# Retention attention and a PReLU feed-forward on one core: w_in's middle tiles loaded and cast in smaller pieces, three loads cut at partition 120

## The chip, the cores and the metric

The kernel runs on one core of a Trainium2 chip. A core has a matrix engine (TensorE, in the profile PE, its weight loads PEld), a vector engine (VectorE, DVE), a scalar engine (ScalarE, ACT), a general engine (GpSimd, POOL) and a sync engine (SyncE, SP), which issues most of the transfers between main memory and the on-chip memory of 128 partitions. Sixteen DMA engines carry these transfers. Each engine runs its own instructions in order and waits on semaphores for the others. The metric is device time in microseconds (us), lower is better; the kernel before was run three times.

## The reference

The reference computes retention attention for 4 batches, 8 heads, 768 positions and head size 64, and puts its result through a feed-forward layer.

```python
gamma = 1.0 - 2.0 ** (-5.0 - np.arange(H, dtype=np.float32))
scale = 1.0 / np.sqrt(D)
for t in range(S):
    state = gamma[None, :, None, None] * state + np.einsum('bhd,bhe->bhde', k[:, :, t], v[:, :, t])
    y[:, :, t] = scale * np.einsum('bhd,bhde->bhe', q[:, :, t], state)
...
x = np.ascontiguousarray(attn_out.transpose(0, 2, 1, 3)).reshape(B * S, H * D)
...
h = x @ w_in
g = np.maximum(h, 0.0) + alpha * np.minimum(h, 0.0)
return (g @ w_out).astype(np.float32)
```

There are 3072 tokens; w_in is 512 x 2048, w_out 2048 x 512, both in float32, as are all inputs.

## The kernel before

The attention is done in chunks. The 3072 positions are cut into 12 units (u = 0 to 11) of 256 positions, three to a batch. For each unit, `load` (L143) brings k, q and v in float32 as tiles ks, qs and vs. `rescale` (L182) multiplies k and q by powers of gamma and writes them as float16 into the tile kdq; `cast_v` makes the float16 tile vx. `turn_pe` (L222) transposes kdq on PE, eight 128 x 128 pieces for one half of the heads, first those of k and then those of q, into a bank of the accumulator (trb), and ACT copies it to the tile kq. `score_mm`, `masks`, `sum_mm`, `state` and `out_mm` then compute scores, masked scores, the unit's contribution to the state, the state, and the attention's output, which is stored transposed as xT.

The feed-forward works on blocks of two units (512 tokens). `ffn1` (L615) multiplies w_in's sixteen column tiles of 128 with xT, four matmuls to a tile and 512 tokens (hps, L629); ACT and DVE then apply the PReLU, into the tile gt. For block 0 it starts with tiles 0 to 3 for one unit at a time (`apart=4`), and goes on with tiles 4 to 15 in order. `ffn2` multiplies gt with w_out (ops). From block 1 on, seven products in place of eight are used for the second matrix.

The order on each engine is written by hand: the code is laid out in the order in which each engine is to do it, and `tick(gen, m)` puts m matmuls of a feed-forward generator between pieces of the attention. So PE has unit 2's transposes (`turn_pe(2, 0, 5)`, L1082) five matmuls after the end of block 0's `ffn1`, and cannot go on until POOL has rescaled unit 2's k and q.

The change concerns how w_in gets in. `get_wi(lo, hi)` (L960) issues on SP one transfer with tiles lo to hi - 1, into a staging buffer named early that `win_part` (L956) picks: tiles 0-3 and 12-15 share one place, so loads of tiles 12-15 have to wait until tiles 0-3 have been cast. `cast_wi` (L963) converts a range to float16 on POOL, into w_in_all (win). In the program's order SP issues: units 0 and 1; w_in 0, 1, 2-3, 4-5, 6-7, 8-11, 12-13, 14-15; then unit 2 (two halves of k, q, v). POOL does: cast 0, 1, 2-3, 4-5, 6-7; issue of w_out's first quarter (`get_wo(0)`, tile wout, converted on the way); cast 8-9, 10-11, 12-15; rescale of unit 2's k for heads 0-3; issue of w_out's second quarter; k for heads 4-7; q; cast of v. SP's transfers report on eight semaphores in turn, so each transfer is issued only when the one eight places earlier has landed.

Of the kernel before, what the change touches and what calls it, by code (L numbers as in the profile page):

```python
# [22 lines left out]
def kernel(  # L23
# [10 lines left out]
    nc = tc.nc  # L34
# [105 lines left out]
    def rows(x):  # L140
        return slice(64 * x, 64 * x + 64)

    def load(u, parts="kqv"):  # L143
        if u >= NU:
            return
        b, c = divmod(u, UPB)
        t = staged.setdefault(u, {})
        for nm in parts:
            src = {"k": k, "q": q, "v": v}[nm[0]]
            if nm[0] not in t:  # L150
                t[nm[0]] = sbp.tile(
                    [128, H, 2 * D], FP, tag=f"{nm[0]}s", bufs=3, name=f"{nm[0]}s{u}"
                )
            h = slice(0, H) if len(nm) == 1 else slice(4 * int(nm[1]), 4 * int(nm[1]) + 4)
            if u >= SPLIT and nm != "q":
                for x in range(2):
                    for y in range(2):
                        at = U * c + 128 * x + 64 * y
                        nc.sync.dma_start(
                            out=t[nm][rows(x), :, D * y : D * y + D],  # L160
                            in_=src[b, :, at : at + 64, :].rearrange("h p d -> p h d"),
                        )
                continue
            hold(
                nc.sync.dma_start(  # L165
                    out=t[nm[0]][:, h, :],
                    in_=src[b, h, U * c : U * c + U, :].rearrange(
                        "h (p r) d -> p h (r d)", r=2
                    ),
                )  # L170
            )
# [10 lines left out]
    def rescale(eng, u, t, h0, h1):  # L182
        kdq = unit(u)[0]
        at = OQ if t else (O2 if u >= SPLIT else 0)
        return eng.tensor_tensor(  # L185
            out=kdq[:, t, :, h0:h1, :].rearrange("p r h d -> p h r d"),
            in0=staged[u]["kq"[t]][:, h0:h1, :].rearrange("p h (r d) -> p h r d", r=2),
            in1=tab[:, at + 2 * h0 : at + 2 * h1]
            .rearrange("p (h r) -> p h r", r=2)
            .unsqueeze(3)  # L190
            .to_broadcast([128, h1 - h0, 2, D]),
            op=MULT,
        )
# [759 lines left out]
    wi = moe_w_in.rearrange("(hp p) d -> p hp d", p=128)  # L953
    wo = moe_w_out.rearrange("(ft p) d -> p ft d", p=128)

    def win_part(lo, hi):  # L956
        x, y = ((1, 0), (1, 1), (0, 0), (1, 0))[lo // 4]
        return early[x][:, y, :, 128 * (lo % 4) : 128 * (hi - lo + lo % 4)]

    def get_wi(lo, hi):  # L960
        nc.sync.dma_start(out=win_part(lo, hi), in_=wi[:, :, 128 * lo : 128 * hi])  # L961

    def cast_wi(eng, lo, hi):  # L963
        o, i = w_in_all[:, :, 128 * lo : 128 * hi], win_part(lo, hi)
        if eng is nc.scalar:
            return eng.activation(out=o, in_=i, func=COPY, bias=0.0, scale=1.0)
        return eng.tensor_copy(out=o, in_=i)  # L967
# [6 lines left out]
    V, G, A = nc.vector, nc.gpsimd, nc.scalar  # L974
# [1 line left out]
    nc.scalar.dma_start(out=alpha_sb, in_=moe_alpha.rearrange("(ft p) -> ft p", p=128))  # L976
    load(0, ("k0", "q0", "k1", "q1", "v0", "v1"))
    load(1, ("k0", "q0", "k1", "q1", "v0", "v1"))
    for lo, hi in ((0, 1), (1, 2), (2, 4), (4, 6), (6, 8), (8, 12)):
        get_wi(lo, hi)  # L980
    V.memset(spin, 1.0)
    V.memset(mi, 1.0)
# [3 lines left out]
        out=ident, in_=ident, pattern=[[-1, 128]], compare_op=EQUAL, fill=0.0,  # L986
# [4 lines left out]
        out=m, in_=m, pattern=[[-1, 2], [1, 2], [2, 64]], compare_op=NOT_LESS,  # L991
        fill=0.0, base=0, channel_multiplier=-2,
    )
    for lo, n in ((0, 64), (256, 32)):
        m = mj[rows(0), lo : lo + 4 * n].rearrange("p (a i t) -> p a i t", a=2, i=2)
        G.affine_select(
            out=m, in_=m, pattern=[[0, 2], [1, 2], [2, n]], compare_op=NOT_LESS,
# [7 lines left out]
        out=mi[rows(1), 0:640], in_=mi[rows(0), 0:640], func=COPY, bias=0.0, scale=1.0  # L1005
# [13 lines left out]
        out=aps[:, 0:NFT], in_=alpha_sb, identity=tab[0:NFT, OI : OI + NFT]  # L1019
# [3 lines left out]
        out=oma_sb, in0=aps[:, 0:NFT], scalar1=-1.0, scalar2=1.0, op0=MULT, op1=ADD  # L1023
# [26 lines left out]
    state(1, 0, V, "ga")  # L1050
    cast_wi(G, 2, 4)
    get_wi(12, 14)
    get_wi(14, 16)
    load(2, ("k0", "k1", "q", "v"))
    score_mm(1, 1, (0, 1))
# [6 lines left out]
    get_wo(0)  # L1062
    cast_wi(G, 8, 10)
    cast_wi(G, 10, 12)
    cast_wi(G, 12, 16)
    rescale(G, 2, 0, 0, 4)
    get_wo(1)
    rescale(G, 2, 0, 4, 8)
# [225 lines left out]
```

## Time and profile before

| | before |
|---|---|
| median of three runs | 199.02 us (198.73 to 199.23) |
| span of the profiled execution | 199.2 us (its own time is not given beside it) |
| PE busy | 190.3 us, 96% |
| DVE, ACT, POOL busy | 156.4, 114.5, 105.1 us |
| read from and written to main memory | 27.31 MB, 6.29 MB |
| granted TensorE clock | 1.000 over the span |

The span runs from the first to the last instruction. The busy time of an engine says little on the end by itself: what counts is which engine waits for what in which stretch. In the rows of the time line, the first number is the start in us from the span's start, the second the duration; xN says how many instructions are merged; in brackets stands how long the engine was idle before and what ended that. SPq rows are issues on SP: their duration is that of the issue, not of the transfer.

### The profile page before, as it was taken

The page shows a single profiled execution, that of the slowest core. Times are in us where ns is not written, and L with a number is a line of the kernel's source. Part 1 is how long each engine was busy: PE and PEld are TensorE (multiplying, and loading weights), DVE is VectorE, ACT ScalarE, POOL GpSimd, SP SyncE. Part 2 cuts the span into 40 slices and gives each one's busy share as a digit, 9 for nine tenths or more (in the row PEclk, how much of TensorE's full clock was granted, in tenths as well). Part 3 has the DMA queues.
Part 4 walks back from the last instruction along what each step waited for, and adds up shares of the span by engine and source line. Part 5 has one row for each costly group of instructions (what it writes and reads, how often), then busy time and mean ns, then how long its engine had stood idle before and what let it go on. Part 6 is the DMA issues. An engine that isn't in the chain of part 4 may idle for free.

```text
span 199.2 us, 6049 instructions
## 1 busy us (share of the span) xinstructions
PE 190.3 (96%) x2517; PEld 128.1 (64%) x2517; DVE 156.4 (79%) x258; ACT 114.5 (57%) x197; POOL 105.1 (53%) x111
## 2 busy tenths in 40 slices
PE   6788979899999999999999999999999999999993
PEld 2456524458548588844598744688644788865882
DVE  6699977236788999379989289987389998899983
ACT  4455754437368658476557576557476476688110
POOL 3197678389477724990067990066980081039400
PEclk9999999999999999999999999999999999999999
DMA  5999996999978999899786999916975110400014
GB/s 156 325 328 368 376 252 144 246 253 161 229 174 198 244 236 243 223 321 200 167 204 174 294 194 211 240 60 143 328 120 127 29 56 3 158 3 0 0 53 158
DMA packets 89449, 36.85 MB, mean 185 GB/s; under 512 B 57920, under 2 KB 87632, under 8 KB 89424
## 3 DMA queue, kind: packets, MB, share of 16 engines
q1 hardware_dynamic: 87136, 34.35, 66.2%
q0 software_dynamic: 2112, 2.10, 6.7%
q8 instruction: 19, 0.31, 0.6%
q10 hardware_dynamic: 176, 0.04, 0.2%
q14 instruction: 6, 0.05, 0.1%
HBM read 27.31 MB, written 6.29 MB: 169 GB/s over the span
## 4 chain that ended last, share of the span: by engine, by line
PE 80%; DMA 9%; SPq 5%; POOL 3%; ACT 1%; issue 1%; DVE 0%
PE hps L629 28%; PE ox L846 16%; PE oy L846 13%; PE ops L798 7%; DMA ks<-in_k_dram 6%; SPq L165 4%; PE hps L712 3%; DMA early<-in_moe_w_in_dram 3%; PE sp L752 3%; POOL kdq L185 2%; PE trb L230 1%; PE st L284 1%; PE y L532 1%; PE sca L465 1%; PE ov L846 1%; SPq L961 1%
## 5 line engine op out<-in xcount | busy, mean ns | idle before, releaser
L629 PE MATMUL hps<-xT,win 128*128 128x512 f16 (+1 forms) x384 | 71.3, 344 | 1.5 <-POOL win L967 1.5
L642 DVE SCALAR_TENSOR_TENSOR gt<-hm,oma,hps 128x512 f16<-128x512 f32 (+1 forms) x96 | 59.5, 655 | 15.2 <-ACT hm L640 6.5
L640 ACT ACTIVATE hm<-hps 128x512 f32<-128x512 f32 x80 | 47.6, 597 | 27.6 <-PE hps L629 25.6
L629 PEld LDWEIGHTS <-win 128*128 128x128 f16 x384 | 37.1, 98 | 33.4 <-POOL win L967 2.6
L846 PEld LDWEIGHTS <-gs 128*128 128x128 f16 x320 | 31.0, 98 | 3.7
L846 PEld LDWEIGHTS <-gt 128*128 128x128 f16 x240 | 22.8, 98 | 4.2
L333 POOL CAST tg<-tm 64x256 f16<-64x256 f32 x12 | 4.8, 396 | 35.0 <-DVE tm L301 22.5
L185 POOL TENSOR_TENSOR kdq<-ks,tab 128x1024 f16<-128x1024 f32 (+1 forms) x12 | 20.2, 1687 | 3.6 <-DMA vs<-in_v_dram 2.6
L185 POOL TENSOR_TENSOR kdq<-qs,tab 128x1024 f16<-128x1024 f32 (+1 forms) x11 | 20.1, 1823 | 2.7 <-DVE wsum L571 2.3
L846 PE MATMUL ox<-wout,gt 128*128 128x256 f16 x144 | 17.3, 273 | 0.0
L555 ACT ACTIVATE xT<-y 128x512 f16<-128x512 f32 x22 | 14.9, 743 | 4.0 <-PE y L532 3.0
L846 PE MATMUL oy<-wsum,gs 128*128 128x256 f16 x144 | 17.2, 272 | 0.0
L201 POOL CAST vx<-vs 128x1024 f16<-128x1024 f32 (+1 forms) x13 | 12.5, 970 | 5.5 <-DMA vs<-in_v_dram 5.5
L798 PE MATMUL ops<-wout,gt 128*128 128x512 f16 x64 | 15.3, 380 | 0.0
L612 DVE TENSOR_TENSOR gs<-gt 128x1024 f16<-128x1024 f16 (+1 forms) x14 | 13.0, 933 | 0.2
L866 ACT ACTIVATE cu<-oy 128x512 f32<-128x512 f32 x10 | 6.0, 597 | 10.6 <-PE oy L846 10.1
L236 ACT ACTIVATE kq<-trb 128x1024 f16<-128x1024 f16 x8 | 8.2, 1023 | 6.7 <-PE trb L230 6.6
L313 POOL TENSOR_TENSOR tf<-ss,tab 128x256 f32<-128x256 f32 x10 | 10.3, 1028 | 2.5 <-DVE ss L312 1.3
L662 POOL TENSOR_SCALAR hn<-qc,oma 128x256 f32<-128x256 f32 x4 | 4.5, 1139 | 12.5 <-DVE qc L774 12.4
L423 POOL TENSOR_TENSOR tf<-ss,tab 128x256 f32<-128x256 f32 x6 | 5.8, 974 | 9.1 <-DVE ss L422 9.1
L870 DVE TENSOR_TENSOR os<-ox,cu 128x512 f32<-128x512 f32 x5 | 3.4, 687 | 9.1 <-PE ox L846 9.1
L967 POOL CAST win<-early 128x1024 f16<-128x1024 f32 (+2 forms) x8 | 8.2, 1039 | 3.7 <-DMA early<-in_moe_w_in_dram 3.6
(116 smaller groups left out, 289.2 us busy)
## 6 DMA issues: line engine op xcount, KB each, us to landing
qs<-in_q_dram SPq DMA_DIRECT2D x10, 512.0 KB, 4.7
ks<-in_k_dram SPq DMA_DIRECT2D x32, 128.0 KB, 3.4
vs<-in_v_dram SPq DMA_DIRECT2D x32, 128.0 KB, 4.3
early<-in_moe_w_in_dram SPq DMA_DIRECT2D x5, 512.0 KB, 7.6
out_dram<-os SPq DMA_DIRECT2D x9, 256.0 KB, 2.6
wout<-in_moe_w_out_dram POOLq DMA_DIRECT2D x4, 512.0 KB, 6.4
out_dram<-ot SPq DMA_DIRECT2D x4, 512.0 KB, 3.6
ks<-in_k_dram SPq DMA_DIRECT2D x6, 256.0 KB, 4.8
```

What stands on the lines that cost most here:

```text
L185: return eng.tensor_tensor(out=kdq[:, t, :, h0:h1, :].rearrange("p r h d -> p h r d"), in0=staged[u]["kq"[t]][:, h0:h1, :].rearrange("p h ...
L201: eng.tensor_copy(out=o, in_=i)
L236: nc.scalar.activation(out=kq.rearrange("p (x a) i -> p x a i", x=4)[:, :, 2 * hh : 2 * hh + 2, :], in_=trb.rearrange("p (x a i) -> p x a ...
L313: nc.gpsimd.tensor_tensor(out=t, in0=ss, in1=dec, op=MULT)
L555: nc.scalar.activation(out=o, in_=i, func=COPY, bias=0.0, scale=1.0,)
L612: last_g.append(nc.vector.tensor_tensor(out=o, in0=a, in1=b, op=op))
L629: nc.tensor.matmul(out=hps[:, f, :].rearrange("p (u t) -> p u t", t=U), lhsT=w_in_all[:, hp, 128 * (f0 + f) : 128 * (f0 + f) + 128], rhs=x ...
L640: nc.scalar.activation(out=hm, in_=hps, func=RELU, bias=0.0, scale=-1.0)
L642: nc.vector.scalar_tensor_tensor(out=gt[:, f0 + f, U * lo : U * hi], in0=hm[:, f, :], scalar=oma_sb[:, f0 + f : f0 + f + 1], in1=hps[:, f, :],
L798: nc.tensor.matmul(out=opss[tq], lhsT=gt[:, ft, 128 * tq : 128 * tq + 128], rhs=w_out_all[:, ft, :], start=(ft == 0), stop=(ft == NFT - 1),)
L846: nc.tensor.matmul(out=o[1][m], lhsT=lhs(f, m), rhs=rhs(f), start=(first and f == 0 and (m == 0 or o[0] is None)), stop=(f == HF - 1), ski ...
L967: return eng.tensor_copy(out=o, in_=i)
```

## The change

Tiles 8-11 are loaded by two transfers, 8-9 and 10-11, in place of one. The cast of tiles 12-15 becomes two instructions. The loads of tiles 6-7, 10-11 and 14-15 are each made by two transfers, one for partitions 0 to 119 and one for partitions 120 to 127. Nothing else is changed; the bytes moved and what is computed are the same.

```diff
     def get_wi(lo, hi):
-        nc.sync.dma_start(out=win_part(lo, hi), in_=wi[:, :, 128 * lo : 128 * hi])
+        for p0, p1 in ((0, 120), (120, 128)) if lo in (6, 10, 14) else ((0, 128),):
+            nc.sync.dma_start(
+                out=win_part(lo, hi)[p0:p1], in_=wi[p0:p1, :, 128 * lo : 128 * hi]
+            )
...
-    for lo, hi in ((0, 1), (1, 2), (2, 4), (4, 6), (6, 8), (8, 12)):
+    for lo, hi in ((0, 1), (1, 2), (2, 4), (4, 6), (6, 8), (8, 10), (10, 12)):
         get_wi(lo, hi)
...
     cast_wi(G, 8, 10)
     cast_wi(G, 10, 12)
-    cast_wi(G, 12, 16)
+    cast_wi(G, 12, 14)
+    cast_wi(G, 14, 16)
     rescale(G, 2, 0, 0, 4)
```

On SP, from the load of tiles 6-7 to unit 2's loads, the program before has these transfers. DMAHW0 to DMAHW7 are the eight semaphores of the transfers, Pool is POOL's own; a wait that an earlier one covers is left out by the compiler.

```order
L961 DMA early<-in_moe_w_in_dram 128x4x256 [waits DMAHW2_49]
L961 DMA early<-in_moe_w_in_dram 128x4x512 [waits DMAHW3_49]
L961 DMA early<-in_moe_w_in_dram 128x4x256 [waits DMAHW6_49,DMAHW7_49,DMAHW4_49,Pool_49]
L961 DMA early<-in_moe_w_in_dram 128x4x256 [waits DMAHW5_49,DMAHW0_49,Pool_49]
L165 DMA ks_390<-in_k_dram 128x4x128 x2
L165 DMA qs_393<-in_q_dram 128x8x128
L165 DMA vs_395<-in_v_dram 128x8x128 [waits DMAHW1_49]
```

The same place now:

```order
L962 DMA early<-in_moe_w_in_dram 120x4x256 [waits DMAHW2_49]
L962 DMA early<-in_moe_w_in_dram 8x4x256 [waits DMAHW3_49]
L962 DMA early<-in_moe_w_in_dram 128x4x256 [waits DMAHW4_49]
L962 DMA early<-in_moe_w_in_dram 120x4x256 [waits DMAHW5_49]
L962 DMA early<-in_moe_w_in_dram 8x4x256 [waits DMAHW6_49]
L962 DMA early<-in_moe_w_in_dram 128x4x256 [waits DMAHW7_49,Pool_49]
L962 DMA early<-in_moe_w_in_dram 120x4x256 [waits DMAHW0_49,Pool_49]
L962 DMA early<-in_moe_w_in_dram 8x4x256 [waits DMAHW1_49]
L165 DMA ks_394<-in_k_dram 128x4x128 [waits DMAHW2_49]
L165 DMA ks_394<-in_k_dram 128x4x128 [waits DMAHW3_49]
L165 DMA qs_397<-in_q_dram 128x8x128 [waits DMAHW4_49]
L165 DMA vs_399<-in_v_dram 128x8x128 [waits DMAHW5_49]
```

Four transfers stand ahead of unit 2's k that did not stand there, and both halves of k and the q now wait for a transfer eight places back: k's halves for the two parts of tiles 6-7, q for tiles 8-9, v for the first part of tiles 10-11.

On POOL, from w_out's first issue to the rescale of unit 2's k, before:

```order
L971 DMA wout<-in_moe_w_out_dram 128x4x512
L967 CAST win<-early 128x4x256 [waits DMAHW3_49]
L967 CAST win<-early 128x4x256
L967 CAST win<-early 128x4x512 [waits DMAHW5_49,DMAHW4_49]
L185 TENSOR_TENSOR kdq_440<-ks_390,tab 128x4x2x64 [waits DMAHW6_49]
```

And now:

```order
L974 DMA wout<-in_moe_w_out_dram 128x4x512
L970 CAST win<-early 128x4x256 [waits DMAHW4_49]
L970 CAST win<-early 128x4x256 [waits DMAHW6_49,DMAHW5_49]
L970 CAST win<-early 128x4x256 [waits DMAHW7_49]
L970 CAST win<-early 128x4x256 [waits DMAHW1_49,DMAHW0_49]
L185 TENSOR_TENSOR kdq_445<-ks_394,tab 128x4x2x64 [waits DMAHW2_49]
```

Each cast of two tiles now waits for its own load alone; before, tiles 8-9 waited for the load of four, and tiles 12-13 for that of 14-15.

## The prediction

> **What bounds the kernel now.** I read the page first: TensorE (PE) is busy for 96% of the span and most of the chain that ended last.
>
> ```profile
> span 199.2 us, 6049 instructions
> PE 190.3 (96%) x2517; PEld 128.1 (64%) x2517; DVE 156.4 (79%) x258; ACT 114.5 (57%) x197; POOL 105.1 (53%) x111
> ...
> GB/s 156 325 328 368 376 252 144 246 253 161 229 174 198 244 236 243 223 321 200 167 204 174 294 194 211 240 60 143 328 120 127 29 56 3 158 3 0 0 53 158
> ...
> q8 instruction: 19, 0.31, 0.6%
> ...
> PE 80%; DMA 9%; SPq 5%; POOL 3%; ACT 1%; issue 1%; DVE 0%
> ```
>
> Only an edit that removes PE idle time can pay, so I asked next where PE is idle: a table of stretches (us, then busy time of PE, PEld, DVE, ACT and POOL with counts, granted clock, DMA share, GB/s).
>
> ```profile
> 18.00:36.00 18.00, 15.78 (x102) 8.05 (x96) 13.87 (x23) 10.15 (x18) 13.60 (x14) 1.00 0.98 269
> 36.00:60.00 24.00, 24.00 (x322) 14.74 (x321) 14.03 (x26) 12.45 (x20) 15.59 (x12) 1.00 0.96 214
> 60.00:84.00 24.00, 24.00 (x386) 19.50 (x384) 19.02 (x34) 16.51 (x30) 15.42 (x14) 1.00 0.96 226
> ```
>
> From 36 us on PE has no idle time and full clock; from 18 to 36 us it lacks 18.00 - 15.78 = 2.22 us. This is block 0's first matrix product, which runs beside the loads of w_in that the change touches. PE and POOL there, in order of time (start, duration, idle before and what ended it):
>
> ```profile
> 18.79 6.29 PE L629 MATMUL hps<-xT,win 128*128 128x256 f16 x40 [0.30 <-POOL win L967]
> 25.61 3.63 PE L629 MATMUL hps<-xT,win 128*128 128x512 f16 x16 [0.53 <-POOL win L967]
> 29.88 3.63 PE L629 MATMUL hps<-xT,win 128*128 128x512 f16 x16 [0.64 <-POOL win L967]
> 33.34 1.24 PE L798 MATMUL ops<-wout,gt 128*128 128x512 f16 x5
> 34.42 0.39 PE L230 MATMUL trb<-mi,kdq 128*128 128x128 f16 x4
> 35.56 0.40 PE L230 MATMUL trb<-mi,kdq 128*128 128x128 f16 x4 [0.75 <-POOL kdq L185]
> ```
>
> ```profile
> 19.98 2.02 POOL L967 CAST win<-early 128x1024 f16<-128x1024 f32 x2
> 21.95 0.99 POOL L971 DMA_DIRECT2D wout<-in_moe_w_out_dram  x1
> 24.52 2.02 POOL L967 CAST win<-early 128x1024 f16<-128x1024 f32 x2 [1.57 <-DMA early<-in_moe_w_in_dram]
> 27.93 1.89 POOL L967 CAST win<-early 128x2048 f16<-128x2048 f32 x1 [1.39 <-DMA early<-in_moe_w_in_dram]
> 30.78 1.04 POOL L185 TENSOR_TENSOR kdq<-ks,tab 128x512 f16<-128x512 f32 x1 [0.95 <-DMA ks<-in_k_dram]
> 31.77 0.81 POOL L971 DMA_DIRECT2D wout<-in_moe_w_out_dram  x1
> 32.59 1.06 POOL L185 TENSOR_TENSOR kdq<-ks,tab 128x512 f16<-128x512 f32 x1
> 33.60 1.90 POOL L185 TENSOR_TENSOR kdq<-qs,tab 128x1024 f16<-128x1024 f32 x1
> ```
>
> PE waits four times for POOL: 0.30 (tiles 2-3), 0.53 (tiles 8-9), 0.64 (tiles 12-15), 0.75 (unit 2's second transposes, which need its rescaled q). POOL in turn waits three times for a landing. The chain that ended last names only the last of these and what is behind it:
>
> ```profile
> 18.76 0.37 SPq L961
> ...
> 19.17 11.53 DMA ks<-in_k_dram
> 30.70 0.08 issue
> 30.78 1.04 POOL kdq L185
> ```
>
> So k of unit 2 lands at 30.70 and everything up to PE's 35.56 hangs on it; the cast waits ahead of it are not on the chain. Without an earlier k, time saved at 25.61 and 29.88 is only waited for at 35.56. Why is k so late? The bytes ahead of it are k, q, v of units 0 and 1 (6 x 0.524 MB), w_in (4.194 MB) and its own 0.262: 7.60 MB. The GB/s row, in slices of 4.98 us, sums over five slices (156 + 325 + 328 + 368 + 376) to 1553 x 4.98 us = 7.73 MB at 24.9 us. The sixteen DMA engines together had moved that much by then, and k was whole 5.8 us later. It isn't mean bandwidth, then, but single engines. No view prints each engine's share, but the trace holds the sixteen increments with which each load reports its landing (us; the packet times are medians of the same record):
>
> ```
> load                 first  15th   last   last - 15th
> k half 0 of unit 0    3.39   4.05   4.11   0.06
> w_in tiles 4-5       16.65  18.42  19.00   0.58
> w_in tiles 6-7       18.28  19.82  20.41   0.59
> w_in tiles 8-11      20.86  22.37  24.46   2.09
> w_in tiles 12-13     22.22  23.69  25.72   2.03
> w_in tiles 14-15     23.59  25.07  27.81   2.74
> k half 0 of unit 2   24.33  25.86  30.70   4.84
> q of unit 2          29.14  30.74  33.01   2.27
> packets: 1 KB 46 ns, 2 KB 84 ns; one 16 KB packet on q8, at 21.50 for 931 ns
> ```
>
> Fifteen shares of k are there at 25.86; one engine brings the last at 30.70. The instruction fetch (q8 above, a single packet of one engine) falls in the stretch where the lag jumps from 0.59 to 2.09, and w_out's first load, issued at 21.95, shares the late engine after 25 us while the others have already finished k.
>
> **The change part by part.** *Three loads (tiles 6-7, 10-11, 14-15) as 120 + 8 partitions.* A load of 128 partitions goes to sixteen engines, eight partitions (32 packets of 1 KB) each. If the shares stay whole, 120 partitions make fifteen, and one engine gets nothing: 3 x 32 x 46 ns = 4.42 us less for it ahead of unit 2's k. The eight remaining partitions are one more for up to eight engines: 3 x 4 x 46 ns = 0.55 us. The other seven are untouched.
>
> *Tiles 8-11 as two loads.* The packets halve: 32 x 84 = 2.69 us per engine become 64 x 46 = 2.94, +0.25 us on every engine. Tiles 8-9 land one load earlier.
>
> *Cast of 12-15 as two.* 1.89 us against 2.02 for two (the row of two at 24.52): +0.13 us for POOL, beside PE, and PE needs only the first ahead of tile 12.
>
> *SP.* Four issues more, at 0.37 to 1.19 us each:
>
> ```profile
> L961 SPq DMA_DIRECT2D early<-in_moe_w_in_dram x8: 368/692/1191, 9.9 to 18.8; - x8
> ```
>
> ```profile
> 14.04 1.05 SPq L961 DMA_DIRECT2D early<-in_moe_w_in_dram  x1
> ```
>
> ```profile
> 16.36 0.37 SPq L961 DMA_DIRECT2D early<-in_moe_w_in_dram  x1
> ```
>
> SP is free from 15.09 to 16.36 and from 16.73 to 18.76 (it waits there for POOL's casts to free the buffers), 3.30 us, against 4 x 0.69 = 2.76: hidden. The last load's second part is issued behind 18.76, and since eight completion counters go round, unit 2's k now waits until tiles 6-7 have landed, about 20.0 instead of an issue at 19.17. Its cover is the queue: tiles 14-15 keep fifteen engines busy until 25. A gap would need an issue later than that. I cost it at nothing (bounds: 0 to the 0.8 us of delay).
>
> *What follows if the spared engine is the late one.* Tiles 8-9 land at about 19.82 + 32 x 46 ns + up to 0.18 = 21.5, so POOL casts 8-9 and 10-11 right behind w_out's issue, from 22.95 to 24.97; 12-13 land at 23.69 + 0.25 + 0.37 = 24.3 and are cast by 26.0; 14-15 land at 25.07 + 0.25 + 0.55 = 25.9 and are cast by 27.0. PE asks for tile 8 at 25.08, for 10 at 26.8, 12 at 28.6, 14 at 30.3: the waits of 0.53 and 0.64 go, 1.17 us. Then PE is at unit 2's second transposes at 34.81 - 1.17 = 33.64 (34.42 + 0.39 is where it stops now). k lands at 25.86 + 0.80 = 26.7 at the latest, its second half 0.75 later. POOL: first half of k to 28.1, w_out's second issue to 28.9, second half to 29.9, then q. q's fifteenth share landed at 30.74; + 0.80 gives 31.5 and the rescale (1.90) ends by 33.5, just ahead of PE. The 0.75 goes too. Between the ends (q at 31.5, or still at 33.01 as before) I take the first: the last share was the late engine's.
>
> Behind 36 us the next step of POOL waits for DVE, which waits for PE's sums, so the shift should be kept:
>
> ```profile
> 40.65 0.61 POOL L423 TENSOR_TENSOR tf<-ss,tab 128x256 f32<-128x256 f32 x1 [4.17 <-DVE ss L422]
> ```
>
> Sum: 0.53 + 0.64 + 0.75 = 1.92 us. The profiled span is 199.2, 0.2 above the median of 199.02, with no time of its own shown; 199.02 - 1.92 = **197.1 us**.
>
> The rows do not name the late engine. [...]
>
> [...]
>
> **The rivals.** *The late engine is among the eight that get more.* Then k lands 0.55 + 0.25 = 0.80 us later than 30.70, POOL's chain behind it takes the same 4.8 us, and PE's last wait ends at 36.36: 199.02 + 0.80 = 199.8 us, more if w_out's packets cost the late engine again. It decides as soon as k's landing moves past 30.70. [...]
>
> *It is one of the seven untouched, or the split spares nobody.* The cast waits go, the wait at the transposes grows by as much: 199.0 to 199.3 us. [...]
>
> *The engine is spared, but w_out's loads hold q back.* w_out's second issue moves from 31.77 to about 28, and its packets run beside q and v. With q at 32.5 PE would go on at 34.45 instead of 33.64: 197.9 us; with q at 33.0, 198.4.
>
> **How the numbers follow.** Forecast 0.64, q held back 0.10, nothing spared 0.11, ninth partition on the late engine 0.15. About 0.3% (0.6 us) is what a measurement of this kernel can tell from no change: the first two are faster (0.74), the third the same (0.11), the fourth slower (0.15). The likeliest case alone spans 196.8 (0.30 at tiles 2-3 gone too) to 197.7. To leave no more than 2 in 10 outside, the range goes through the held-back case up to the unchanged one: 196.8 to 199.3 us.
>
> **What the changed profile would show.** Right: unit 2's k landing before 28 us; POOL's casts of tiles 8-15 without idle time of over 0.5 us between them; PE's waits for tiles 8 and 12 gone and the one at the transposes under 0.2; PE's busy time unchanged and the stretch 18 to 36 us shorter by about 1.9. Wrong: k landing at 30 or later, or a new PE wait behind 36 us, for instance for w_out or unit 3, which takes the shift back.

## The result: 3.8% slower

The kernel after takes 207.46 us (median of four runs, 204.98 to 208.21) against 198.88 us (198.15 to 199.23) beside it; the ratio, here and below without runs over 1.5% slower than the fastest of their kernel, is 1.038, 95% interval 1.033 to 1.043. The forecast was 197.1 us, the range ended at 199.3. The profiled execution below took 208.21 us, the longest of the four. In it the granted clock is lower for a while behind 41 us (mean over the span 0.991); two others of the four have much the same mean (0.992), without a trace to say where. The fourth, at 1.000, still has a span of 202.9 us and a time of 204.98, so that dip is only part of the loss.

From the page of the profile after: span, busy times, rates (GB/s in 40 slices, here of 5.16 us), packets, and the chain that ended last by engine:

```profile
span 206.2 us, 6056 instructions
PE 191.8 (93%) x2517; PEld 128.0 (62%) x2517; DVE 156.3 (76%) x258; ACT 114.4 (55%) x197; POOL 105.8 (51%) x112
...
GB/s 154 320 323 255 228 228 262 159 287 176 126 251 196 182 260 206 249 201 308 173 242 174 223 237 201 241 98 153 269 195 127 25 54 7 153 3 0 0 53 150
DMA packets 89998, 36.85 MB, mean 179 GB/s; under 512 B 57957, under 2 KB 88693, under 8 KB 89973
...
PE 78%; DMA 11%; SPq 6%; POOL 2%; ACT 1%; issue 1%; DVE 0%
```

In the fourth to sixth slices, which begin as the first cut load does, the rate is 228 to 255 GB/s, where before it was 368, 376 and 252. PE's busy time grew by only 1.5 us; most of the rest is idle time, and most of that is in the stage that the change touches (columns as in the prediction: stretch, then PE, PEld, DVE, ACT, POOL, granted clock, DMA share, GB/s):

```profile
18.00:36.00 18.00, 15.08 (x111) 7.35 (x108) 12.62 (x22) 9.56 (x17) 9.10 (x11) 1.00 1.11 235
36.00:60.00 24.00, 20.71 (x258) 13.07 (x257) 9.44 (x20) 9.76 (x14) 16.92 (x13) 0.93 0.92 198
60.00:84.00 24.00, 24.00 (x364) 17.05 (x361) 21.63 (x37) 15.69 (x29) 15.11 (x14) 1.00 0.94 219
```

The DMA share is 1.11, so the engines are not idle: they have more to do for 235 GB/s than before for 269. PE's waits from 16 to 60 us (in all, times, longest):

```profile
PE trb L230 <- POOL kdq L185: 3.3, 1, 3.3
PE hps L629 <- POOL win L970: 3.2, 6, 1.2
```

POOL behind them waits for a landing ahead of nearly each cast and ahead of unit 2's k (start, duration, idle before and its cause):

```profile
24.41 1.04 POOL L970 CAST win<-early 128x1024 f16<-128x1024 f32 x1 [2.25 <-DMA early<-in_moe_w_in_dram]
...
32.95 1.04 POOL L970 CAST win<-early 128x1024 f16<-128x1024 f32 x1 [1.18 <-DMA early<-in_moe_w_in_dram]
35.89 1.04 POOL L185 TENSOR_TENSOR kdq<-ks,tab 128x512 f16<-128x512 f32 x1 [1.89 <-DMA ks<-in_k_dram]
```

And the chain that ended last has two transfers, one behind the other, for 23 us of it:

```profile
12.88 11.48 DMA early<-in_moe_w_in_dram
24.37 11.44 DMA ks<-in_k_dram
35.81 0.08 issue
35.89 1.04 POOL kdq L185
```

The first is the 120-partition part of tiles 6-7. It lands at 24.35 instead of 20.41, and since k may be issued only behind it (the counter), k is issued at 24.37 instead of 19.17 and lands at 35.81. The trace's packets on SP's queue say why (start of the packet; nanoseconds of one, tenth percentile / median / ninetieth):

```
us       before, 1 KB     after, 1 KB      before, 512 B    after, 512 B
14-17    46 / 46 / 46     46 / 46 / 46     27 / 27 / 27     27 / 27 / 27
17-20    46 / 46 / 46     46 / 85 / 114
20-23    46 / 46 / 46     62 / 76 / 94
23-26    46 / 46 / 46     61 / 72 / 86     27 / 27 / 27
26-29                     60 / 74 / 96     27 / 27 / 27     27 / 35 / 49
29-32                     59 / 71 / 84     27 / 27 / 27     34 / 40 / 51
```

From the start of the first cut load the median packet takes 1.3 to 1.8 times as long, that of unit 2's whole loads too (the 512 B packets from 26 to 32 us), and this ends only when the last cut load is through (its last share lands at 32.90).

The lower clock behind 41 us (the same view in finer stretches) is the other part:

```profile
36.00:41.00 5.00, 1.71 (x14) 0.85 (x13) 1.25 (x2) 0.58 (x1) 4.98 (x5) 1.00 0.73 159
41.00:44.00 3.00, 3.00 (x33) 1.72 (x31) 0.81 (x2) 1.02 (x1) 0.59 (x1) 0.67 0.96 235
44.00:47.00 3.00, 3.00 (x42) 1.37 (x40) 0.72 (x2) 1.02 (x1) 0.00 (x0) 0.76 1.15 343
```

At 0.67 and 0.76 of the clock for 3 us each, 3 x 0.33 + 3 x 0.24 = 1.7 us are lost (an estimate from these two rows), right behind the 3.3 us in which PE stood.

### The profile page after: what moved, and what is told of

It is laid out like the page before. It is cut to its first block, busy times and chain, and to the rows that moved or that the text cites. A ratio compares the mean times of both kernels' runs of the same rounds, so it can differ in the third digit from the quotient of the medians.

```text
span 206.2 us, 6056 instructions
## 1 busy us (share of the span) xinstructions
PE 191.8 (93%) x2517; PEld 128.0 (62%) x2517; DVE 156.3 (76%) x258; ACT 114.4 (55%) x197; POOL 105.8 (51%) x112
## 4 chain that ended last, share of the span: by engine, by line
PE 78%; DMA 11%; SPq 6%; POOL 2%; ACT 1%; issue 1%; DVE 0%
PE hps L629 27%; PE ox L846 16%; PE oy L846 12%; PE ops L798 7%; DMA early<-in_moe_w_in_dram 6%; DMA ks<-in_k_dram 6%; SPq L165 4%; PE hps L712 3%; PE sp L752 3%; POOL kdq L185 2%; SPq L962 1%; PE trb L230 1%; PE sca L465 1%; PE st L284 1%; PE y L532 1%; PE ov L846 1%
## 5 line engine op out<-in xcount | busy, mean ns | idle before, releaser
L798 PE MATMUL ops<-wout,gt 128*128 128x512 f16 x64 | 16.3, 397 | 0.0
L970 POOL CAST win<-early 128x1024 f16<-128x1024 f32 (+1 forms) x9 | 8.6, 958 | 8.1 <-DMA early<-in_moe_w_in_dram 8.0
L482 DVE TENSOR_TENSOR m<-sca,mi 128x512 f16<-128x512 f32 x8 | 5.5, 683 | 7.2 <-PE scb L465 7.2
```

The lines of the kernel that those rows point to most:

```text
L798: nc.tensor.matmul(out=opss[tq], lhsT=gt[:, ft, 128 * tq : 128 * tq + 128], rhs=w_out_all[:, ft, :], start=(ft == 0), stop=(ft == NFT - 1),)
```

## The experiments

The theory after the result: loads that are cut by partitions slow the packets of everything in flight. The rivals: the number of transfers (twelve where there were eight), the smaller tiles and casts, or one fixed late engine. Beside e1 to e4 the kernel before took 199.21 us, beside e6 to e8 198.58, beside e9 to e11 198.98 (medians).

**e1_tiles: the change without the cuts.** Against the kernel after:

```diff
-        for p0, p1 in ((0, 120), (120, 128)) if lo in (6, 10, 14) else ((0, 128),):
-            nc.sync.dma_start(
-                out=win_part(lo, hi)[p0:p1], in_=wi[p0:p1, :, 128 * lo : 128 * hi]
-            )
+        nc.sync.dma_start(out=win_part(lo, hi), in_=wi[:, :, 128 * lo : 128 * hi])
```

> Tiles 8-11 as two loads and the cast of 12-15 as two, with no load cut by partitions: five transfers fewer... that is, nine w_in loads in place of twelve. Theory P (the cut by partitions makes packets slow: in the changed kernel 1 KB packets take 46 ns until 17 us and 70 to 90 ns from 17 to 31 us): packets stay at 46 ns, unit 2's k lands near 30.7 us, PE's waits for tiles 8 and 12 shrink and the wait at unit 2's transposes grows by as much, time 198.6 to 199.4 us. Theory T (the halved packets and the extra casts cost the time): near the changed kernel, 205 to 207 us.

Measured: 199.93 us, ratio 1.003 (0.999 to 1.007) to before; 1 KB packets take 46 ns. The time is 0.5 us above the range expected, and the first half of unit 2's k landed at 27.71, not near 30.7; the packets and the ratio are those of the first theory. The tiles and casts cost and gain nothing that can be measured.

**e2_cut_only: the cuts without the rest.** Before, with tiles 6-7 and 14-15 cut:

```diff
-        nc.sync.dma_start(out=win_part(lo, hi), in_=wi[:, :, 128 * lo : 128 * hi])
+        for p0, p1 in ((0, 120), (120, 128)) if lo in (6, 14) else ((0, 128),):
+            nc.sync.dma_start(
+                out=win_part(lo, hi)[p0:p1], in_=wi[p0:p1, :, 128 * lo : 128 * hi]
+            )
```

> The kernel before with only the loads of tiles 6-7 and 14-15 cut at partition 120; tiles 8-11 stay one load and 12-15 one cast. Theory P: slow packets from 17 us on, w_in's tiles and unit 2's k later by some 2 to 4 us, time 202 to 206 us. Theory T: no change, 198.6 to 199.4 us. Theory N (it is the number of transfers, each of which waits for the one eight places earlier): two more transfers, a part of the loss, 200 to 203 us, with packets at 46 ns.

Measured: 203.91 us, ratio 1.022 (1.019 to 1.027). From 17 to 20 us 1 KB packets take 79 ns (median) and the first 2 KB packets, those of the whole load of tiles 8-11, 157, where before they took 46 and 84; the later 2 KB packets take 105 and 94. PE's waits from 16 to 60 us:

```profile
PE hps L629 <- POOL win L970: 5.3, 5, 1.8
PE trb L230 <- POOL kdq L185: 0.6, 1, 0.6
```

The loss is there without the split of tiles 8-11; here PE pays it at the casts.

**e3_cut64: the cut at another place.** The change, with halves:

```diff
-        for p0, p1 in ((0, 120), (120, 128)) if lo in (6, 10, 14) else ((0, 128),):
+        for p0, p1 in ((0, 64), (64, 128)) if lo in (6, 10, 14) else ((0, 128),):
```

> The changed kernel with the cut at partition 64 in place of 120: the same twelve transfers, each half with the same number of increments as a whole load. If the slow packets come from the count of fifteen or from the small second part, they are gone: 46 ns, time 198.6 to 199.6 us. If they come from any cut by partitions (theory P in its wide form), packets of the cut loads are slow again, up to twice 46 ns, time 203 to 208 us. [...]

Measured: 207.35 us, ratio 1.030 (1.022 to 1.039); 1 KB packets 67 to 73 ns from 17 to 29 us. Two equal parts cost about what 120 + 8 costs, so it isn't the small part that does it, nor a share of 15.

**e4_rows31: as many transfers, no cut by partitions.** The change, each of the three loads in two by w_in's rows, three quarters and one quarter:

```diff
-        for p0, p1 in ((0, 120), (120, 128)) if lo in (6, 10, 14) else ((0, 128),):
+        for h0, h1 in ((0, 3), (3, 4)) if lo in (6, 10, 14) else ((0, 4),):
...
-                out=win_part(lo, hi)[p0:p1], in_=wi[p0:p1, :, 128 * lo : 128 * hi]
+                out=win_part(lo, hi)[:, h0:h1], in_=wi[:, h0:h1, 128 * lo : 128 * hi]
```

> The changed kernel with the same three loads each made by two transfers of all 128 partitions, three quarters and one quarter of the rows of w_in, packets of 1 KB as before: the same number of transfers as in the changed kernel, in the same order with the same waits for counters. Theory N: 204 to 208 us. Theory P: packets at 46 ns, time like that of the kernel with no cut, 198.6 to 199.6 us.

Measured: 199.97 us, ratio 1.004 (1.001 to 1.007); packets 46 ns. The time is 0.4 us above the range expected. The same twelve transfers on the same eight counters cost 0.4%, by the interval 0.7 at most, so the number of transfers falls as the cause of the 3.8%.

**e8_one_cut: one cut alone.** The change, with only tiles 14-15 cut:

```diff
-        for p0, p1 in ((0, 120), (120, 128)) if lo in (6, 10, 14) else ((0, 128),):
+        for p0, p1 in ((0, 120), (120, 128)) if lo == 14 else ((0, 128),):
```

> The changed kernel with only the load of tiles 14-15 cut at partition 120. Theory P: packets run slow only from where that load reaches the engines, about 23 us, until 26 us; unit 2's k 1 to 2.5 us later than without a cut; time 200 to 202.5 us, about a third of the loss. If the loss needs several cut loads behind each other, 198.6 to 199.6 us.

Measured: 202.43 us, ratio 1.017 (1.011 to 1.022). 1 KB packets take 46 ns up to 23 us and 73 (46 to 99) from 23 to 26, where the one cut load runs; the rate there is 240 GB/s, where before had 326. PE then waits at unit 2's transposes:

```profile
PE trb L230 <- POOL kdq L185: 2.4, 1, 2.4
PE ops L798 <- DMA wout<-in_moe_w_out_dram: 0.4, 1, 0.4
```

The slow packets begin with the cut load, wherever it is put.

**e6_probe: which engine is late.** Before, with four tiny loads of 16, 15, 8 and 4 partitions behind w_in's, to read the landing of single engines (in after, a load of 8 partitions reports with eight increments and one of 128 with sixteen), and five loads at the end, one at a time, into tiles that nothing uses:

```diff
+    probe = sbp.tile([16, 4, 16], FP, tag="probe", name="probe")
+    for i, n in enumerate((16, 15, 8, 4)):
+        nc.sync.dma_start(out=probe[0:n, i], in_=moe_w_in[0:n, 16 * i : 16 * i + 16])
...
+        if not more:
+            quiet = sbp.tile([128, 4, 256], FP, tag="quiet", name="quiet")
+            for p in (slice(0, 128), slice(0, 120), slice(0, 64), slice(0, 8), slice(0, 32, 4)):
+                nc.sync.dma_start(out=quiet[p], in_=wi[p, :, 0:256])
```

> The kernel before with nine extra loads of w_in's values into unused tiles, the work else untouched. [...] Five quiet ones stand at the end, when the DMA queues are nearly empty, each issued after the one before has landed: 128, 120, 64 and 8 neighbouring partitions and 8 partitions at a distance of 4. If slow packets come from the shape of the transfer itself, the 1 KB packets of 120, 64 and 8 neighbouring partitions take 60 ns or more, those of 128 take 46 ns. If they come from engines that are out of step in a full queue, all take 46 ns. [...]

Measured: 198.52 us in one run (before beside it 198.58). There was no late engine to name: the fifteenth share of tiles 14-15 came at 24.83 and the last at 24.84, and the first half of unit 2's k was whole at 25.66. PE had no wait from 16 to 60 us. Of the loads at the end, one in flight at a time, four took 46 ns a packet (median). The one of 120 partitions took 46 up to 175 us and 56 to 79 (medians of quarters of a us) behind it, until 176.4, with no other load in flight: the load of 120 was slow by itself there, and those of 64 and of 8 were not.

**e9_before: before once more, with another profile.** No edit.

> The kernel before, unchanged, for a second profile. The profiled executions of the runs so far have a span 1.7 to 2.0 us below their own time, so the execution that the prediction was read from, with its span of 199.2, took about 201 us and was not a typical one (median 198.6 to 199.2). If its waits for late loads belong to that execution alone, this profile has a span of about 197 us, unit 2's k lands before 29 us and PE's waits for POOL between 18 and 36 us sum to less than 1.2 us, against 2.2. If they are the kernel's own, the waits are 1.9 to 2.5 us again.

Measured: 198.78 us, span 197.1. The stretch of the first product and POOL in it:

```profile
18.00:36.00 18.00, 17.85 (x133) 9.55 (x122) 14.31 (x25) 11.47 (x19) 13.41 (x13) 1.00 1.09 291
```

```profile
22.53 2.04 POOL L967 CAST win<-early 128x1024 f16<-128x1024 f32 x2
25.18 1.90 POOL L967 CAST win<-early 128x2048 f16<-128x2048 f32 x1 [0.61 <-DMA early<-in_moe_w_in_dram]
27.04 1.04 POOL L185 TENSOR_TENSOR kdq<-ks,tab 128x512 f16<-128x512 f32 x1
```

PE lacks 0.15 us of 18, not 2.22; the first half of unit 2's k is there at 25.81 and POOL rescales it at 27.04 without a wait. The program of before runs through this stage unchanged in e11 and e12 too: PE lacks 0.43 and 0.83 us there. So the 2.22 us with the four waits on which the prediction was built were those of one execution; in the three others it is 0.15 to 0.83.

**e7_ticks and e10_ticks32: is there time to win at unit 2's transposes?** e1 with the transposes three matmuls later; e10 has the last pair of lines too, so that w_out's third quarter is still asked for after 32 matmuls, as before:

```diff
-    tick(gen, 5)
+    tick(gen, 8)
     turn_pe(2, 0, 5)
...
-    tick(gen, 6)
+    tick(gen, 5)
     score_mm(2, 1, (6, 7))
...
-    tick(gen, 8)
+    tick(gen, 6)
```

> No cut by partitions; tiles 8-11 as two loads and 12-15 as two casts as in the change, and unit 2's transposes put three matmuls of the next product later (8, 6, 5 in place of 5, 6, 6). If the wait at unit 2's transposes is what took back the time that the smaller loads and casts saved (0.5 us in the run without a cut, 0.75 before), it goes: PE has no wait for POOL between 20 and 40 us, and the time is 197.4 to 198.6 us. If the gain is taken back elsewhere (a wait for w_out or the next scores), it stays at 198.6 to 199.6 us.

> As the run with the transposes three matmuls later, with the same 32 matmuls ahead of w_out's third quarter as before (8, 6, 5, 6, 7 in place of 5, 6, 6, 8, 7). The wait of 4.2 us for w_out's third quarter is gone. If a wait for unit 2's q is left in a typical execution without the cut, the time is 0.3 to 1 us below the kernel before; if typical executions have none, it is the same within 0.5 us, 198.4 to 199.4 us.

Measured: e7 207.33 us, ratio 1.039 (1.033 to 1.045), a miss; e10 199.13 us, ratio 1.0015 (0.999 to 1.004). In e7 a new wait took the place of the other:

```profile
PE ops L798 <- DMA wout<-in_moe_w_out_dram: 4.2, 1, 4.2
PE trb L230 <- POOL kdq L185: 1.0, 1, 1.0
```

Two of `ffn2`'s matmuls more ahead of w_out's third load bring PE to its third quarter before that has landed. With their number kept, no gain is left either: nothing tried here beats the kernel before.

**e11_quiet: the partition pattern by itself.** Before, with loads of w_in at the end into tiles that nothing uses, several in flight:

```diff
+        if not more:
+            def quiet(i, pieces):
+                t = sbp.tile([128, 4, 256], FP, tag=("kdq", "kq")[i % 2], bufs=3, name="quiet")
+                for p0, p1 in pieces:
+                    nc.sync.dma_start(out=t[p0:p1], in_=wi[p0:p1, :, 0:256])
+            for i in range(4):
+                quiet(i, ((0, 128),))
+            for i in range(4):
+                quiet(i, ((0, 64), (64, 128)))
+            for i in range(2):
+                quiet(i, [(16 * x, 16 * x + 16) for x in range(8)])
+            for i in range(3):
+                quiet(i, ((0, 120), (120, 128)))
```

> The kernel before with loads of w_in's values into unused tiles at its end, where the queues are nearly empty, in four stretches, 1 KB packets throughout, several loads in flight so that the engines are full: four loads of 128 partitions; four in halves of 64; two in eighths of 16; three in 120 and 8. If the slow packets come from which partitions the engines write at the same time, 128 gives 46 ns, 64 and 120 give about 75 ns (both as in the cut kernels), and 16 gives more again, up to 150 ns. If they come from what surrounds the loads at the start (other loads, w_out, POOL), all take 46 ns. [...]

Measured: 46 ns (median) in the loads of 128, 73 to 75 in the halves, 55 to 72 in 120 + 8. The eighths gave 46 with a ninetieth percentile of up to 253, at a DMA share of 0.56 to 0.58 from 186 to 194 us: the engines were not full (an eighth is 64 KB, and SP's 34 issues took 26.03 us, with their waits 0.77 each), so this dose was a miss. Whether memory's side or the writing side is slow stayed open, since the loads differ in both.

**e12_ports: the same addresses, other partitions.** Before, with these loads behind its last store, into tiles that nothing uses (of the loads of 32 and 16 partitions, every second one starts 32 partitions higher):

```diff
+    for wide, starts in (
+        (128, 8 * (0,)), (64, 4 * (0,)), (64, 4 * (0,)), (32, (0, 32, 0, 32)),
+        (32, (0, 32, 0, 32)), (16, (0, 32)), (16, (0, 32)), (128, 8 * (0,)),
+    ):
+        t, r = sbp.tile([128, 16, 256], FP, tag="gt", bufs=2, name="quiet"), 256 // wide
+        for j, p in enumerate(starts):
+            slot = j * r if wide >= 64 else j // 2 * r
+            rows, col = slice(256 * (j % 2), 256 * (j % 2) + 256), 256 * (j // 2)
+            nc.sync.dma_start(
+                out=t[p : p + wide, slot : slot + r],
+                in_=moe_w_in[rows, col : col + 256].rearrange("(p r) d -> p r d", p=wide),
+            )
```

> Before, with loads of w_in behind its last store, into tiles that nothing uses (so its time says nothing; only the packets are looked at). Every load reads 256 rows x 1 KB, in the same order of addresses, and fills 128 partitions (two rows to each), the lower 64 (four), 32 (eight) or 16 (sixteen); then 128 again. What differs is the partitions written alone. If the slow packets come from the order in which main memory is read: 46 ns in all five stretches. If they come from any load that gives an engine fewer than eight partitions: 72 to 75 ns in the three narrow ones alike. If they come from engines that write one another's partitions, in proportion to their number: 46, about 75, 150 and 300 ns. [...]

Measured, in the stretches of 128, 64, 32, 16 and again 128 partitions (columns as above; DMA share and GB/s are the last two):

```profile
198.00:204.00 6.00, 0.00 (x0) 0.00 (x0) 0.00 (x0) 0.00 (x0) 0.00 (x0) 0.56 0.93 293
206.00:214.00 8.00, 0.00 (x0) 0.00 (x0) 0.00 (x0) 0.00 (x0) 0.00 (x0) 0.50 1.12 210
216.00:223.00 7.00, 0.00 (x0) 0.00 (x0) 0.00 (x0) 0.00 (x0) 0.00 (x0) 0.50 1.12 208
225.00:228.00 3.00, 0.00 (x0) 0.00 (x0) 0.00 (x0) 0.00 (x0) 0.00 (x0) 0.50 1.01 102
236.00:239.00 3.00, 0.00 (x0) 0.00 (x0) 0.00 (x0) 0.00 (x0) 0.00 (x0) 0.50 1.05 360
```

```
partitions     128    64    32    16    128
1 KB packet    46     84    85   155     46 ns (median)
```

The engines are full in all of them (a DMA share of 0.93 to 1.12). The order in which memory is read, the same in all five, falls. So does a fixed price for narrow loads, since 16 cost twice what 32 cost, and so does a price by the partitions of one load, since 64 and 32 cost the same. A price by the partitions written at one time isn't ruled out here: neighbouring loads overlap (of two loads of 32, the second's first share lands at 216.43, the first's last at 217.40), and as they alternate, 64 partitions are then written in the stretch of 32 as well, and 32 in that of 16. Against it stand the loads of 120 + 8 above, which are slow too. What sets the price in e12 is not shown: measured are 46 ns for 128 partitions, 84 and 85 for 64 and 32, and 155 for 16.

## Why the prediction was wrong

**The step that failed** is the price of the cut: "If the shares stay whole, 120 partitions make fifteen, and one engine gets nothing: 3 x 32 x 46 ns = 4.42 us less for it". The number of shares is as supposed: in after, a part of 120 reports with fifteen increments, one of 8 with eight. But the 46 ns do not hold. With 71 to 85 ns the spared engine has little to gain and all the others lose: what moved at 386 GB/s from 20 to 23 us moves at 230. The landing of tiles 6-7 is 3.9 us late (24.35 against 20.41), that of k 5.1 (35.81 against 30.70), though the engines moved the same bytes. It isn't one engine: k's fifteenth share lands at 34.39 against 25.86. Against e9, with tiles 6-7 at 19.66 and k at 25.81, they are 4.7 and 10.0 us late.

That the late engine is the one that a load of 120 leaves out, on which the 197.1 us rests, is shown by no run: e6 was to tell, and there no engine was late.

That cutting by partitions makes the packets slow is shown by e1 to e4 and e8. Why it does is not shown. In e12 the narrow loads are slow (84 to 155 ns), but a load of 120 is not narrow, and alone in flight its packets took 56 to 79 ns from 175 to 176.4 us (e6), where those of one of 64 took 46; no run here shows which engine wrote which partition.

**The base was untypical.** "The profiled span is 199.2, 0.2 above the median of 199.02, with no time of its own shown". Of the 48 executions of before that ran beside the experiments, 46 have a span 1.67 to 2.05 us below their time (e9: 197.1 and 198.78), so a span of 199.2 belonged to an execution of about 201 us. The 1.92 us of waits that the sum took off were mostly its own. An execution with a span near 197.1, like e9, would have shown that PE lacks 0.15 us in this stage, and that there is almost nothing to gain in it.

**The late engine.** It was real in that execution (4.84 us between fifteenth and last share of k) and absent in e6 and e9 (0.03 and 0.10). It is no accident of one execution, though: for one half of unit 2's k, e12 has 3.74 us, e7 3.47 and e1 2.86. What made it is open. The instruction fetch that the prediction saw at its start does not do so alone: e6 has the same packet at 20.56 us, for 879 ns, and no w_in or k load behind it lags by more than 0.13.

**Tiles 8-11 and the casts** ("+0.25 us" and "+0.13 us", hidden): right within what e1 can tell (1.003, 0.999 to 1.007).

**SP**: "I cost it at nothing (bounds: 0 to the 0.8 us of delay)". The counters hold k as described, but behind tiles 6-7 at 24.35, so the delay of the issue is 24.37 - 19.17 = 5.2 us. It follows from the slow packets. Its cover held: k joined a queue whose tiles 14-15 landed only at 32.90, and the engines were full (a DMA share of 1.03 to 1.20 in each us from 20 to 35), so no loss by it shows. With 46 ns packets, in e4, the same counters cost 0.4% with all else.

**The rivals.** The slower one had the right sign and the right sentence ("it decides as soon as k's landing moves past 30.70"), but its mechanism, a ninth partition for the late engine, and its price, 0.80 us, were wrong: k moved by 5.1 us with the packets slow, those of its own whole load too (512 B: 35 to 40 ns in place of 27). The second ended at no change, 199.0 to 199.3 us; the fastest of the four runs took 204.98.

**The signs named beforehand**: "k landing at 30 or later" was the mark of a wrong prediction, and k landed at 35.81. Three of POOL's four casts of tiles 8-15 waited, for 0.93 to 1.22 us; the waits for tiles 8 and 12 grew to six of 3.2 us in all, and the one at the transposes from 0.75 to 3.3.

**Where the time went**: 6.5 us of PE waits from 16 to 41 us and 1.7 us of lower clock, 8.2 of the 206.2 - 197.1 = 9.1 us between this execution and e9; 0.9 us lies elsewhere, 0.4 of it ahead of 16 us, where no cut load runs yet (PE busy for 11.84 us there, in e9 for 12.21); the rest was not followed. In the one execution after with full clock the span is 202.9, 5.8 above e9.

## What to carry to other kernels

Cutting a load by partitions to rebalance the DMA engines slowed the packets in flight in each kernel here that did it (1 KB: medians of 67 to 85 ns in place of 46 in after, e2, e3 and e8), and cost 3.8%, where the waits that it was to remove were 1.92 us in one execution and mostly less in others; cutting by rows (e4) or columns (e1), with all 128 partitions in each transfer, left them at 46 ns. Take the time of one packet under the new pattern as the unknown of such an edit, and bound it from the slowest shape at hand. Before summing waits of a few tenths, see whether span and time belong together and whether a second execution has the same waits.

## What was not expected of the hardware

- Of two loads of the same bytes, one to 128 partitions ran at 293 to 360 GB/s and one to 64 or 32 at 208 to 210, to 16 at 102 (e12); cut loads slowed a whole load in flight beside them (e2: 2 KB packets 157 ns in place of 84, from 17 to 20 us).
- One engine was 4.84 us late in one execution of the kernel before and on time in two others like it (0.03 us in e6, 0.10 in e9).
- Where PE stood for 3.3 us in one piece, its granted clock fell to 0.50 for a time: in after from 42.0 to 45.4 us, which cost 1.7 us, half as much again as the wait; in e3 from 36.5, still inside the wait, to 43.3, which cost 2.7 us of work. In e7, with 4.2 us in one piece, it fell too (46.9 to 50.3). Below, for e3, the row of the time line and three stretches from within the wait on, with the granted clock third from the end; in e8, the last two fences, the piece is 2.45 us and the clock stays full:

```profile
37.94 0.61 PE L230 MATMUL trb<-mi,kdq 128*128 128x128 f16 x4 [3.29 <-POOL kdq L185]
```

```profile
37.00:40.00 3.00, 2.06 (x8) 1.01 (x9) 0.00 (x0) 1.02 (x1) 1.86 (x2) 0.50 1.11 191
40.00:42.00 2.00, 2.00 (x23) 0.94 (x22) 0.27 (x1) 0.00 (x0) 0.00 (x0) 0.50 1.09 324
42.00:45.00 3.00, 3.00 (x46) 1.71 (x44) 1.06 (x3) 1.02 (x1) 0.00 (x0) 0.79 1.18 333
```

```profile
36.54 0.40 PE L230 MATMUL trb<-mi,kdq 128*128 128x128 f16 x4 [2.45 <-POOL kdq L185]
```

```profile
37.00:40.00 3.00, 3.00 (x35) 1.59 (x34) 1.29 (x2) 1.83 (x2) 0.47 (x1) 1.00 0.93 229
```

e2's 5.3 us in five waits, the longest 1.8, leave it at 1.00 too. So in these profiles the waits of 3.29 us (after, e3) and of 4.2 (e7) went with a clock of 0.50 and cost more than their length, and those of 2.45 (e8) and 1.8 (e2) did not.
